# Two heads' scores in two neighbouring PSUM banks, one exponential over 1024 columns

## The chip, the cores and the metric

The kernel runs on one NeuronCore of one Trainium2 chip. The metric is the device time of one execution in microseconds, as the median of several runs. Next to it stands one profiled execution, whose span (first to last instruction) the views divide up.

## What is computed

A pre-norm transformer block on 2048 rows of 512 columns, in fp32: attention with 32 heads of 16 columns and no mask, then a feed-forward part with 1792 hidden columns and SiLU.

```python
def _A_ref(x, wqkv, wo):
    B, S, D = x.shape
    H = 32; Dh = D // H
    qkv = (lambda x, *d: x.transpose(*d))((x @ wqkv).reshape(B, S, 3, H, Dh), 2, 0, 3, 1, 4)
    q, k, v = qkv[0], qkv[1], qkv[2]
    scale = Dh ** -0.5
    scores = jnp.einsum("bhqd,bhkd->bhqk", q, k) * scale
    p = _softmax(scores, axis=-1)
    o = jnp.einsum("bhqk,bhkd->bhqd", p, v)
    return (lambda x, *d: x.transpose(*d))(o, 0, 2, 1, 3).reshape(B, S, D) @ wo
...
def _B_ref(x, w1, w2):
    h = jnp.einsum("bsd,df->bsf", x, w1)
    h = _silu(h)
    out = jnp.einsum("bsf,fd->bsd", h, w2)
    return out
...
h = x + _A_ref(_layernorm(x, axis=-1), A_wqkv, A_wo)
h2 = h + _B_ref(_layernorm(h, axis=-1), B_w1, B_w2)
```

## The kernel before

**Stages.** A first stage normalizes x, turns it and projects q, k and v. Q and k are stored as fp16 parts in DRAM, v stays in SBUF (`va`). Then the attention runs over 32 *items*. An item is a block of 512 query rows (four blocks, eight items each) and four heads; its 2048 keys are cut into 16 chunks. One item and one chunk make a *group*, so there are 512 groups. After the first group of items 9, 17 and 25 the feed-forward part of the finished block is run (`finish_block`, `mlp`), and that of the last block at the end (`finish_last`).

**A group.** The loop from line 690 writes the order out by hand; TensorE (PE), ScalarE (ACT), VectorE (DVE) and the DMA queue of SyncE (SP) each keep program order. Per group:

- `scores(g, k)` (line 459) for four heads: a matmul with 64 rows and 512 columns into a bank, and an exponential of 512 columns from that bank into a tile `pt` (ACT). Heads alternate between the lower and the upper half of PE's rows.
- `one_max` (line 257) after the first n of the four: a maximum needs the scores of later items, 128 queries by 512 keys, in an orientation of its own (a matmul with 48 rows on the *other* half of PE's rows, then a `tensor_reduce` on DVE). 64 of them make an item. `maxima(g)` (line 674) plans n, at most 3 a group, from what is done and from two constants, `BESIDE` and `AHEAD`.
- `values(g - 2)` (line 470): four fp32 matmuls of `pt` with `va`, 17 output rows each, side by side in the one bank `pv`. Each is two passes in the trace.

**Around the groups.** After an item's 64th maximum `finish_max` (line 210) reduces them to `nm` on DVE and splits it on POOL; two groups later `place_max` (line 223) transposes it on PE into a bank `ps_n`, copies it on ACT (`mt`), and sends it with four DMAs into the rows of `qs` that the item's scores read. After an item's last `values`, `finish_item` (line 485) copies `pv` on ACT (`pvs`), and the next item's `values` can begin only then. In items 8, 16 and 24, groups 10 to 15 carry `output` (line 618): twelve matmuls of the output projection into `ps_wo` (`project_rows`), an addition and statistics on DVE (`add_rows`), a normalization, and four transposes into `ps_tr` (`turn`, line 161), which ACT copies and from which DVE takes the low part.

**Banks.** PSUM has eight banks. From line 437 they are cut into rings: `st` with four banks (scores, `ps_n`, `ps_wo`, `ps_tr`, and the sums of `mlp`), `sm` with three (maxima; in `mlp` also `ps_n`), and `pv`. A ring hands its banks out in turn, so that a new user waits for the last reader of the oldest one.

**Feed-forward.** `mlp` (line 570) takes 14 chunks of 128 hidden columns; every eighth of its products is followed by a burst of three maxima.

Of the kernel before, what the change touches and what calls it, by code (L numbers as in the profile page):

```python
# [9 lines left out]
F32 = mybir.dt.float32  # L10
# [9 lines left out]
P = 128  # L20
# [17 lines left out]


LAG = 2  # L40
PTS = 12

RING = 5

# [1 line left out]
ITEMS = NB * H // 4  # L46

WAIT = 2
AHEAD = 4


BESIDE = 126
OUTPUT = 9

BESIDE_A = 7, 4
# [4 lines left out]
def attention_mlp_kernel(ctx: ExitStack, tc: tile.TileContext, x, wqkv, wo, w1, w2, out):  # L60
# [59 lines left out]
    def bank(name, kind="st", dtype=F32):  # L120
        return banks[kind].tile([P, 512], dtype, tag=kind, name=name)

    ident = const.tile([P, P], F32, name="ident")
    make_identity(nc, ident)
    ident_h = const.tile([P, P], F16, name="ident_h")
# [32 lines left out]
    def normalize(dst, rows, mv, rs):  # L158
        dve("tensor_scalar", dst, rows, mv[:, 0:1], rs, op0=ALU.subtract, op1=ALU.mult)

    def turn(src, dst_h, dst_l):

        ps = bank("ps_tr").rearrange("p (c n) -> p c n", n=P)
        for c in range(4):
            tr(ps[:, c, :], src[:, c * P:(c + 1) * P], ident)
        act("copy", dst_h, ps)
        low(dst_l, ps, dst_h)
# [54 lines left out]

    def place_max(i, ns):

        ps = bank("ps_n", "sm" if at["mlp"] else "st", F16)
        tr(ps[:32, :P], ns.rearrange("p a b -> p (a b)"), ident_h)
        mt = small.tile([32, P], F16, name="mt")
        pin(nc.scalar.copy(mt, ps[:32, :P]))
        for j in range(2):
            for r in range(2):  # L230
                dst = qs[i % RING][64 * j + 48 + r:64 * j + 49 + r].rearrange("o a n -> o (a n)")
                pin(nc.sync.dma_start(dst.rearrange("o (a b) -> o a b", b=P),
                                      mt[16 * r + 8 * j:16 * r + 8 * j + 8, :]))
        placed.add(i)
# [2 lines left out]
    todo = {(i, j): [(i, kb, qt, a, j) for kb in range(4) for a in range(2) for qt in range(4)]  # L237
            for i in range(ITEMS) for j in range(2)}
    END = 64 * ITEMS
    at = {"item": 0, "done": 0, "half": 0, "products": 0, "step": 0, "due": 0, "mlp": False}  # L240
    agenda = {}

    def soon(steps, fn, *a):
# [190 lines left out]
                    load_k(2 + n // 4, n % 4)  # L434


    open_banks(ctx, 1, st=4, sm=3, pv=1)
    pv = bank("pv", "pv")
    pin(nc.vector.memset(pv, 0.0))
    cpool = ctx.enter_context(tc.tile_pool(name="cpool", bufs=1, side="right"))  # L440
# [8 lines left out]
    groups = ITEMS * KC  # L449
    pts, den = {}, {}  # L450

    def scores(g, k):

        i, c = divmod(g, KC)
        a, j = HEADS[k]
        assert i in placed
        ps = bank("ps_s")
        mm(ps, ks[i % RING][64 * j:64 * j + 64, a, c * P:(c + 1) * P], qs[i % RING][64 * j:64 * j + 64, a, :],
           start=True, stop=True)
        pts[g, k] = bp.tile([P, 512], F32, name="pt")  # L460
        act("activation", pts[g, k], ps, AF.Exp, scale=qk_f)

    def values(g):
        i, c = divmod(g, KC)
        for k in range(4):
            a, j = HEADS[k]
            mm(pv[32 * k:32 * k + DH + 1, :], va[:, c, 4 * (i % 8) + 2 * a + j, :], pts.pop((g, k)),
               start=c == 0, stop=c == KC - 1)
        if c == KC - 1:
            finish_item(i)  # L470

# [93 lines left out]
        return statistics(h)  # L565

    def turn_rows(t):
        turn(hx.pop(t), hth[:, :, t * P:(t + 1) * P], htl[:, :, t * P:(t + 1) * P])

    def mlp(b, beside):  # L570
        engine = "pool" if beside else "dve"

        first = bank("ps_w1")
        acc = [bank("ps_acc") for _ in range(3)]

        def second(f, gh, gl):
            w2h, w2l = ws.pop(("w2", f))
            if f == 0:
                acc.append(bank("ps_acc"))
            for t in range(4):  # L580
                weave(product(acc[t], lambda c: gh[:, t * P:(t + 1) * P], lambda c: gl[:, t * P:(t + 1) * P],
                              lambda c: w2h, lambda c: w2l, 1, start=f == 0, stop=f == FC - 1),
                      beside if f < FC - 1 else None)
                if f == FC - 1:
                    n = 4 * b + t
                    h = rows_of(b, t)
                    dve("tensor_tensor", h, acc[t], h, ALU.add)
                    dma(out[n * P:(n + 1) * P, :], h)

        last = None  # L590
        for f in range(FC):
            tick()
            if f < 2:
                at["products"] = 12
            load_weights("w1", f + 2)
            load_weights("w2", f + 1)
            w1h, w1l = (w.rearrange("p (c n) -> p c n", n=P) for w in ws.pop(("w1", f)))
            split_weights("w1", f + 1, engine)
            split_weights("w2", f, engine)
            ps = pv if f else first  # L600
            weave(product(ps, lambda c: w1h[:, c, :], lambda c: w1l[:, c, :],
                          lambda c: hth[:, c, :], lambda c: htl[:, c, :], DC), beside)
            g, gh, gl = (bp.tile([P, 512], dt, tag="pt", name=name)
                         for name, dt in (("g", F32), ("gh", F32R), ("gl", F32R)))
            act("activation", g, ps, AF.Silu)
            act("copy", gh, g)
            low(gl, g, gh)
            if last:
                second(*last)
            last = (f, gh, gl)  # L610
        if b < NB - 1:

            act("activation", small.tile([P, 1], F32, name="sw"), ident[:, :1], AF.Exp)
        second(*last)
# [3 lines left out]
    def output(b, n):  # L618

        if n < 4:  # L620
            ps = bank("ps_wo")
            run(project_rows(n, ps))
            found[n] = add_rows(b, n, ps)
        if 0 < n < 5:
            normalize(hx[n - 1], rows_of(b, n - 1), *found.pop(n - 1))
        if 1 < n < 6:
            turn_rows(n - 2)

    def finish_block(b, pending):

        act("activation", small.tile([P, 1], F32, name="sw"), ident[:, :1], AF.Silu)
        for g in pending:
            values(g)
        at["mlp"] = True
        mlp(b, BESIDE_C)
        at["mlp"] = False

    def finish_last(pending):

        b, i = NB - 1, ITEMS - 1  # L640
        O = ot[b % 2]
        for t in range(4):
            os[t] = [bp.tile([P, DC, P], F32R, tag="pt", name=name) for name in ("oh", "ol")]
            act("copy", os[t][0][:, :3], O[:, t, :3])
            low(os[t][1][:, :3], O[:, t, :3], os[t][0][:, :3])
        for g in pending:
            values(g)
        agenda.clear()
        sums(i)
        invert(i)  # L650
        spread(i)
        split_weights("w1", 0, "dve")
        ps = [bank("ps_wo") for _ in range(4)]
        for t in range(4):
            run(project_rows(t, ps[t], range(3), stop=False))
        divide(i)
        for t in range(4):
            act("copy", os[t][0][:, 3:], O[:, t, 3:])
            low(os[t][1][:, 3:], O[:, t, 3:], os[t][0][:, 3:])
        act("activation", small.tile([P, 1], F32, name="sw"), ident[:, :1], AF.Silu)  # L660
        found = {}
        for t in range(4):
            run(project_rows(t, ps[t], [3], start=False))
            found[t] = add_rows(b, t, ps[t])
            if t > 0:
                normalize(hx[t - 1], rows_of(b, t - 1), *found[t - 1])
        normalize(hx[3], rows_of(b, 3), *found[3])
        for t in range(4):
            turn_rows(t)
        mlp(b, None)  # L670
# [19 lines left out]
    for g in range(groups):  # L690
        tick()
        i, c = divmod(g, KC)
        if g in marks:
            finish_block(i // 8 - 1, (g - 2, g - 1))
        if i + RING - 1 < ITEMS and 6 <= c < 14:
            (load_k if c % 2 else load_q)(i + RING - 1, c // 2 - 3)
        if g < DC:
            w = gp.tile([P, 512], F32, tag="w", name="w", bufs=4)
            dma(w, wo[g * P:(g + 1) * P, :])
            soon(8, split_wo, g, w)  # L700
        if i in (8, 16, 24):
            b, n = i // 8 - 1, c - OUTPUT
            if c < 4:
                load_rows(b, c)
            if c in first_weights:
                load_weights(*first_weights[c])
            if 0 <= n < 4:
                split_rows(b, n)
            if c == 13:
                split_weights("w1", 0, "pool")  # L710
        if g == groups - 4:
            for t in range(4):
                load_rows(NB - 1, t)
            for w in first_weights.values():
                load_weights(*w)
        n = maxima(g)
        for m in range(4):
            k = m ^ (g % 2)
            scores(g, k)
            if m < n:  # L720
                one_max(1 - HEADS[k][1])
        if i in (8, 16, 24) and c > OUTPUT:
            output(i // 8 - 1, c - OUTPUT - 1)
        if g - LAG >= 0 and not (g in marks or g - 1 in marks):
            values(g - LAG)
    assert at["done"] == END
# [33 lines left out]
```

## Time and profile before

| what | value |
|---|---|
| median of 3 runs | 1741.3 us (1739.5 to 1748.47) |
| profiled execution, its own time | 1747.01 us |
| its span; mean granted clock | 1745.2 us; 0.987 |
| PE, DVE, ACT, POOL busy | 1696.8, 1453.6, 1258.9, 229.5 us |
| groups of block 0 and item 8 (207.6 to 486.2 us) | 278.60 us; PE 275.74, DVE 257.79, ACT 277.34 busy |
| next block (627.7 to 877 us) | 249.30 us; PE 247.53, DVE 233.21, ACT 245.21 busy |
| next block (1017 to 1272 us) | 255.00 us; PE 249.33, DVE 233.41, ACT 245.51 busy |
| last block (1411 to 1632 us) | 221.00 us; PE 218.67, DVE 173.94, ACT 220.08 busy |

The first stage fills what lies before 207.6 us, and the feed-forward parts with the output projections what lies between these stretches. An engine counts as busy from an instruction's start to its end, with what overlaps counted once; ends of matmuls are modelled. In a row of the timeline stand start, length, engine, line, operation, output and inputs, shape, the number of merged instructions, and in brackets the idle time before and what ended it. A row with a count over one runs from the first one's start to the last one's end, and matmuls on the two halves of PE's rows overlap.

### The profile page before, as it was taken

How to read it: one execution, taken by the hardware profiler on the slowest of the kernel's cores; microseconds unless marked ns; L12 is line 12 of the kernel's file. 1: busy time of each engine (PE TensorE's matmuls, PEld its weight loads, DVE VectorE, ACT ScalarE, POOL GpSimd, SP SyncE). 2: the span in 40 equal slices, each digit the busy share in tenths (PEclk: the TensorE clock that was granted, in tenths of full speed). 3: DMA queues.
4: the chain of work that ended last, by engine and by line, in shares of the span. 5: the costliest groups of instructions: out<-in, count | busy, mean ns of one | idle time of the engine just before them, and what ended most of it. 6: DMA issues, size and time to landing. Idle time of an engine off the chain costs nothing.

```text
span 1745.2 us, 28284 instructions
## 1 busy us (share of the span) xinstructions
PE 1696.8 (97%) x10466; PEld 655.6 (38%) x10466; DVE 1453.6 (83%) x2392; ACT 1258.9 (72%) x2507; POOL 229.5 (13%) x312
## 2 busy tenths in 40 slices
PE   7899999999999999999999999999999999999899
PEld 6665422222245532222245532222245532221377
DVE  6879899999978889999978889999878899995243
ACT  4223499999963269999963369999863279999643
POOL 2112210000033300000033300000033300000000
PEclk9999999999999999999999999999999999999999
DMA  5234311111113111111222111111122111100232
GB/s 183 92 79 145 112 34 46 39 42 44 59 55 93 55 41 38 35 50 36 61 69 82 50 44 35 38 47 38 57 62 84 55 41 39 35 8 11 64 91 73
DMA packets 102211, 103.11 MB, mean 59 GB/s; under 512 B 20344, under 2 KB 78776, under 8 KB 102072
## 3 DMA queue, kind: packets, MB, share of 16 engines
q1 hardware_dynamic: 102072, 101.30, 19.6%
q8 instruction: 82, 1.34, 0.3%
q14 instruction: 57, 0.47, 0.1%
HBM read 77.86 MB, written 17.30 MB: 55 GB/s over the span
## 4 chain that ended last, share of the span: by engine, by line
ACT 45%; PE 44%; DVE 8%; DMA 1%; issue 1%; SPq 1%; POOL 0%; ACTq 0%; POOLq 0%; DVEq 0%
ACT pt L81 44%; PE pv L67 15%; PE ps_acc L67 7%; PE ps_m L67 6%; PE ps_qk L67 6%; DVE mx L206 5%; PE ps_s L67 5%; PE ps_wo L67 2%; PE ps_v L67 2%; DVE gl L84 1%; PE ps_w L67 1%; ACT pvs L81 1%; PE ps_tr L70 1%; DVE st L84 0%; DVE ot L84 0%
## 5 line engine op out<-in xcount | busy, mean ns | idle before, releaser
L206 DVE TENSOR_REDUCE mx<-ps_m 128x1 f32<-128x512 f32 x2048 | 1280.8, 683 | 127.5 <-PE ps_m L67 100.5
L81 ACT ACTIVATE pt<-ps_s 128x512 f32<-128x512 f32 x2048 | 1015.5, 657 | 34.8 <-PE ps_m L67 34.1
L67 PE MATMUL ps_s<-qs,ks 64*128 64x512 f16 x2048 | 552.7, 381 | 14.9 <-DMA qs<-mt 4.7
L67 PE MATMUL pv<-pt,va 128*17 128x512 f32 x4096 | 542.5, 603 | 0.8
L67 PE MATMUL ps_m<-ks,qs 48*128 48x512 f16 x2048 | 526.0, 383 | 2.2 <-DVE mx L206 0.8
L67 PEld LDWEIGHTS <-ks 64*128 64x128 f16 x2048 | 154.7, 95 | 552.3 <-issue 436.4
L67 PEld LDWEIGHTS pv<-pt,va 128*17 128x17 f32 x4096 | 68.7, 95 | 234.5 <-issue 219.7
L67 PEld LDWEIGHTS <-qs 48*128 48x128 f16 x2048 | 121.4, 94 | 77.0 <-issue 74.5
L81 ACT ACTIVATE g<-pv 128x512 f32<-128x512 f32 x52 | 31.0, 597 | 140.5 <-PE pv L67 140.4
L74 POOL TENSOR_SCALAR nm<-nm 128x16 f32<-128x16 f32 x32 | 9.4, 294 | 728.8 <-DVE nm L213 712.1
L67 PE MATMUL ps_acc<-w2h,gh 128*128 128x512 f32 x224 | 92.2, 411 | 0.0
L67 PE MATMUL ps_acc<-w2l,gh 128*128 128x512 f32 x224 | 91.6, 409 | 0.0
L67 PE MATMUL ps_acc<-w2h,gl 128*128 128x512 f32 x224 | 88.2, 394 | 0.0
L84 DVE TENSOR_TENSOR gl<-g,gh 128x512 fp32r<-128x512 f32 x56 | 53.3, 952 | 41.6 <-ACT gh L81 41.6
L67 PE MATMUL pv<-hth,w1l 128*128 128x512 f32 x208 | 86.2, 415 | 0.0
L81 ACT CAST w2h<-w 128x512 fp32r<-128x512 f32 x56 | 34.7, 620 | 70.7 <-PE ps_acc L67 33.9
L67 PE MATMUL pv<-hth,w1h 128*128 128x512 f32 x208 | 83.1, 400 | 0.0
L67 PE MATMUL pv<-htl,w1h 128*128 128x512 f32 x208 | 82.5, 397 | 0.0
L74 POOL TENSOR_TENSOR w1l<-w,w1h 128x512 fp32r<-128x512 f32 x42 | 53.7, 1280 | 154.6 <-ACT w1h L81 138.6
L81 ACT ACTIVATE ks<-ps_qk,qk_s 128x512 f32<-128x512 f32 x24 | 16.5, 688 | 68.2 <-PE ps_qk L67 68.2
L74 POOL TENSOR_TENSOR w2l<-w,w2h 128x512 fp32r<-128x512 f32 x42 | 53.7, 1280 | 50.1 <-ACT w2h L81 50.1
L67 PE MATMUL ps_qk<-xtl,wqk_h 128*128 128x512 f32 x128 | 53.4, 417 | 3.4 <-DVE xtl L84 3.4
(100 smaller groups left out, 1183.0 us busy)
## 6 DMA issues: line engine op xcount, KB each, us to landing
w<-in_B_w_dram SPq DMA_DIRECT2D x112, 256.0 KB
ks<-kd SPq DMA_DIRECT2D x120, 192.0 KB
qs<-qd SPq DMA_DIRECT2D x128, 48.0 KB
kd<-sh SPq DMA_DIRECT2D x16, 256.0 KB
qd<-sh SPq DMA_DIRECT2D x16, 256.0 KB
ot<-pvs SPq DMA_DIRECT2D x128, 32.0 KB
den<-dr SPq DMA_DIRECT2D x128, 32.0 KB
hx<-in_A_x_dram SPq DMA_DIRECT2D x16, 256.0 KB
```

What stands on the lines that cost most here:

```text
L67: tc.keep_in_program_order(nc.tensor.matmul(*a, **k))
L70: tc.keep_in_program_order(nc.tensor.transpose(*a))
L74: tc.keep_in_program_order(getattr(nc.gpsimd, op)(*a, **k))
L81: pin(getattr(nc.scalar, fn)(*a, **k))
L84: pin(getattr(nc.vector, fn)(*a, **k))
L206: pin(nc.vector.tensor_reduce(mx[i][:, j, a, qt, kb:kb + 1], ps, axis=AX.X, op=ALU.max))
```

## The change

Scores of two heads go into one tile of two neighbouring banks, and one exponential of 1024 columns reads both. The ring `st` of four banks becomes a ring `two` of two such tiles; the bytes of `pt` stay (six tiles of twice the size for twelve). A group's order becomes: pair of scores, up to two maxima, pair of scores, `output` if any, third maximum, `values`. `ps_n`, `ps_wo` and `ps_tr` move into the ring `sm` of three banks, which the maxima use. `mlp` and `finish_last` take their four sums from two such tiles. `mlp` runs one more burst of three maxima beside its first chunk (`BESIDE` 129 for 126), and `AHEAD` is 6 for 4.

```diff
-PTS = 12
+PTS = 6
...
-AHEAD = 4
-BESIDE = 126
+AHEAD = 6
+BESIDE = 129
...
+    def two_banks(name):
+        return banks["two"].tile([P, 2, 512], F32, tag="two", name=name)
...
-    def turn(src, dst_h, dst_l):
-        ps = bank("ps_tr").rearrange("p (c n) -> p c n", n=P)
+    def turn(src, dst_h, dst_l, kind="st"):
+        ps = bank("ps_tr", kind).rearrange("p (c n) -> p c n", n=P)
...
-        ps = bank("ps_n", "sm" if at["mlp"] else "st", F16)
+        ps = bank("ps_n", "sm" if "two" in banks else "st", F16)
...
-    open_banks(ctx, 1, st=4, sm=3, pv=1)
+    open_banks(ctx, 1, two=2, sm=3, pv=1)
...
-    def scores(g, k):
+    def scores(g, pair):
         i, c = divmod(g, KC)
-        a, j = HEADS[k]
         assert i in placed
-        ps = bank("ps_s")
-        mm(ps, ks[i % RING][64 * j:64 * j + 64, a, c * P:(c + 1) * P], qs[i % RING][64 * j:64 * j + 64, a, :],
-           start=True, stop=True)
-        pts[g, k] = bp.tile([P, 512], F32, name="pt")
-        act("activation", pts[g, k], ps, AF.Exp, scale=qk_f)
+        ps = two_banks("ps_s")
+        for m in range(2):
+            n = m ^ (g % 2)
+            a, j = HEADS[2 * pair + n]
+            mm(ps[:, n, :], ks[i % RING][64 * j:64 * j + 64, a, c * P:(c + 1) * P],
+               qs[i % RING][64 * j:64 * j + 64, a, :], start=True, stop=True)
+        pts[g, pair] = bp.tile([P, 2, 512], F32, tag="pt", name="pt")
+        act("activation", pts[g, pair], ps, AF.Exp, scale=qk_f)
...
-            mm(pv[32 * k:32 * k + DH + 1, :], va[:, c, 4 * (i % 8) + 2 * a + j, :], pts.pop((g, k)),
-               start=c == 0, stop=c == KC - 1)
+            mm(pv[32 * k:32 * k + DH + 1, :], va[:, c, 4 * (i % 8) + 2 * a + j, :],
+               pts[g, k // 2][:, k % 2, :], start=c == 0, stop=c == KC - 1)
...
-        first = bank("ps_w1")
-        acc = [bank("ps_acc") for _ in range(3)]
+        acc = [ps[:, m, :] for ps in [two_banks("ps_acc") for _ in range(2)] for m in range(2)]
+        first = acc[3]
...
-            if f == 0:
-                acc.append(bank("ps_acc"))
...
+            if beside and f == 0:
+                burst(beside[1])
...
-            g, gh, gl = (bp.tile([P, 512], dt, tag="pt", name=name)
-                         for name, dt in (("g", F32), ("gh", F32R), ("gl", F32R)))
+            g = bp.tile([P, 2, 512], F32, tag="pt", name="g")[:, 0, :]
+            gs = bp.tile([P, 2, 512], F32R, tag="pt", name="gs")
+            gh, gl = gs[:, 0, :], gs[:, 1, :]
...
-            ps = bank("ps_wo")
+            ps = bank("ps_wo", "sm")
...
-        ps = [bank("ps_wo") for _ in range(4)]
+        ps = [w[:, m, :] for w in [two_banks("ps_wo") for _ in range(2)] for m in range(2)]
...
-        n = maxima(g)
-        for m in range(4):
-            k = m ^ (g % 2)
-            scores(g, k)
-            if m < n:
-                one_max(1 - HEADS[k][1])
+        halves = [HEADS[(m + g) % 2][1] for m in range(maxima(g))]
+        scores(g, 0)
+        for half in halves[:2]:
+            one_max(half)
+        scores(g, 1)
         if i in (8, 16, 24) and c > OUTPUT:
             output(i // 8 - 1, c - OUTPUT - 1)
+        for half in halves[2:]:
+            one_max(half)
         if g - LAG >= 0 and not (g in marks or g - 1 in marks):
             values(g - LAG)
```

More of the change, by code (lines that the diff above doesn't have):

```diff
@@ L239, in attention_mlp_kernel @@
     END = 64 * ITEMS
-    at = {"item": 0, "done": 0, "half": 0, "products": 0, "step": 0, "due": 0, "mlp": False}
+    at = {"item": 0, "done": 0, "half": 0, "products": 0, "step": 0, "due": 0}
     agenda = {}
@@ L466, in values @@
             a, j = HEADS[k]
-            mm(pv[32 * k:32 * k + DH + 1, :], va[:, c, 4 * (i % 8) + 2 * a + j, :], pts.pop((g, k)),
-               start=c == 0, stop=c == KC - 1)
+            mm(pv[32 * k:32 * k + DH + 1, :], va[:, c, 4 * (i % 8) + 2 * a + j, :],
+               pts[g, k // 2][:, k % 2, :], start=c == 0, stop=c == KC - 1)
+        for pair in range(2):
+            del pts[g, pair]
         if c == KC - 1:
@@ L567, in turn_rows @@
     def turn_rows(t):
-        turn(hx.pop(t), hth[:, :, t * P:(t + 1) * P], htl[:, :, t * P:(t + 1) * P])
+        turn(hx.pop(t), hth[:, :, t * P:(t + 1) * P], htl[:, :, t * P:(t + 1) * P], "sm")
     def mlp(b, beside):
         engine = "pool" if beside else "dve"
-        first = bank("ps_w1")
-        acc = [bank("ps_acc") for _ in range(3)]
+        acc = [ps[:, m, :] for ps in [two_banks("ps_acc") for _ in range(2)] for m in range(2)]
+        first = acc[3]
         def second(f, gh, gl):
             w2h, w2l = ws.pop(("w2", f))
-            if f == 0:
-                acc.append(bank("ps_acc"))
             for t in range(4):
@@ L633, in finish_block @@
             values(g)
-        at["mlp"] = True
         mlp(b, BESIDE_C)
-        at["mlp"] = False
     def finish_last(pending):
@@ L642, in finish_last @@
         for t in range(4):
-            os[t] = [bp.tile([P, DC, P], F32R, tag="pt", name=name) for name in ("oh", "ol")]
+            o = bp.tile([P, 2, DC, P], F32R, tag="pt", name="os")
+            os[t] = o[:, 0], o[:, 1]
             act("copy", os[t][0][:, :3], O[:, t, :3])
```

## The prediction, made before the changed kernel was run

> **What bounds the kernel now.** I read the page first: busy time by engine, then the chain of work that ended last.
>
> ```profile
> PE 1696.8 (97%) x10466; PEld 655.6 (38%) x10466; DVE 1453.6 (83%) x2392; ACT 1258.9 (72%) x2507; POOL 229.5 (13%) x312
> ...
> ACT pt L81 44%; PE pv L67 15%; PE ps_acc L67 7%; PE ps_m L67 6%; PE ps_qk L67 6%; DVE mx L206 5%; PE ps_s L67 5%; PE ps_wo L67 2%; PE ps_v L67 2%; DVE gl L84 1%; PE ps_w L67 1%; ACT pvs L81 1%; PE ps_tr L70 1%; DVE st L84 0%; DVE ot L84 0%
> ...
> L206 DVE TENSOR_REDUCE mx<-ps_m 128x1 f32<-128x512 f32 x2048 | 1280.8, 683 | 127.5 <-PE ps_m L67 100.5
> L81 ACT ACTIVATE pt<-ps_s 128x512 f32<-128x512 f32 x2048 | 1015.5, 657 | 34.8 <-PE ps_m L67 34.1
> ```
>
> The chain names the exponentials (44%), but PE is busy for 97%. Which of the two sets a group's pace is not to be read from shares, so I took the timeline of PE through one ordinary group with three maxima, and of ACT through groups with none.
>
> ```profile
> 704.46 0.39 PE L67 MATMUL ps_s<-qs,ks 64*128 64x512 f16 x1
> 704.46 0.60 PE L67 MATMUL ps_m<-ks,qs 48*128 48x512 f16 x2
> 704.69 0.59 PE L67 MATMUL ps_s<-qs,ks 64*128 64x512 f16 x2
> ...
> 705.13 0.37 PE L67 MATMUL ps_s<-qs,ks 64*128 64x512 f16 x1
> 705.43 1.05 PE L67 MATMUL pv<-pt,va 128*17 128x512 f32 x8
> 706.42 0.39 PE L67 MATMUL ps_s<-qs,ks 64*128 64x512 f16 x1
> ...
> 1612.42 17.85 ACT L81 ACTIVATE pt<-ps_s 128x512 f32<-128x512 f32 x36
> ```
>
> A group lasts 706.42 - 704.46 = 1.96 us. PE fills it: seven short matmuls in four slots of 0.22 (two run side by side on the two halves of the rows, the last alone), `values` 0.97 after the start, and 0.99 to the next group. ACT: 36 exponentials in 17.85 us are one every (17.85 - 0.66) / 35 = 0.491, so four take 1.96 too. **Both limits coincide.** Whatever ACT saves, a group with three maxima cannot be shorter than PE's 1.96. Following the planner's arithmetic, 489 of the 512 groups carry three maxima before, 486 after.
>
> **The steady group.** PE's order after: pair at 0, two maxima at 0.22, pair at 0.45, third maximum at 0.67, `values` at 0.97, next group at 1.96: the same four slots. Nothing is removed on PE. On ACT two instructions replace four; their price isn't in the trace, so I bound it by what columns cost in neighbouring shapes.
>
> ```profile
> L81 ACT CAST gh<-g 128x512 fp32r<-128x512 f32 x56 | 34.8, 621 | 1.8
> L81 ACT ACTIVATE g<-pv 128x512 f32<-128x512 f32 x52 | 31.0, 597 | 140.5 <-PE pv L67 140.4
> L81 ACT ACTIVATE sw<-ident 128x1 f32<-128x1 f32 x7 | 1.4, 203 | 0.1
> L81 ACT CAST oh<-ot 128x128 fp32r<-128x128 f32 x4 | 0.9, 295 | 10.3 <-DVE ot L84 10.3
> ```
>
> ```profile
> 502.89 0.39 PE L67 MATMUL ps_s<-qs,ks 64*128 64x512 f16 x1
> ...
> 503.31 0.60 ACT L81 ACTIVATE pt<-ps_s 128x512 f32<-128x512 f32 x1 [0.20 <-PE ps_m L67]
> ```
>
> Columns cost (597 - 203) / 511 = 0.77 ns or (621 - 295) / 384 = 0.85 ns, so 512 more cost 0.395 to 0.435 us. An exponential by itself takes 0.60; one of 1024 columns then lasts D = 0.995 to 1.035 and comes every I = 0.886 to 0.926. ACT needs 2I = 1.77 to 1.85 a group: some 0.15 idle, the real gain of this change.
>
> But only two tiles exist, and they tie ACT to PE. The first exponential starts 0.42 after its scores (502.89 to 503.31), the second ends at 0.42 + D + I, the next group's second pair may start 0.05 later (bank handed on, shown below), and from there PE needs 1.96 - 0.45 = 1.51 to the next group. Two periods are thus at least 0.42 + D + I + 0.05 + 1.51, or P = (1.98 + D + I) / 2. With D + I = 1.88 to 1.96 that gives 1.93 to 1.97: at PE's own 1.96, and over it by up to 0.01. For some 430 ordinary groups 0 to +4 us; I take **+2**.
>
> The Trainium skill, "ScalarE: Activation LUTs", section "What ACT_TABLE_LOAD costs", gives an ACTIVATE with immediate operands 186 ns plus 0.833 ns a column, overlapping the next by about 93 ns. Estimated from it, D + I is 1.04 + 0.95 = 1.99, P 1.985 and this term +11 us; but for 512 columns it gives one every 520 ns, where the trace has 491, so I keep the rows.
>
> **The end of an item.** Its copy of `pv` stands between exponentials on ACT.
>
> ```profile
> 342.30 0.39 PE L67 MATMUL ps_s<-qs,ks 64*128 64x512 f16 x1
> ...
> 343.36 1.05 PE L67 MATMUL pv<-pt,va 128*17 128x512 f32 x8
> ...
> 346.62 0.39 PE L67 MATMUL ps_s<-qs,ks 64*128 64x512 f16 x1
> ```
>
> ```profile
> 342.69 0.62 ACT L81 COPY pvs<-pv 128x512 f32<-128x512 f32 x1
> 343.15 4.09 ACT L81 ACTIVATE pt<-ps_s 128x512 f32<-128x512 f32 x8
> ```
>
> `pvs` ends at 343.31 and `values` starts at 343.36: this is the 0.05 of handing on. The two groups take 4.32, 0.40 over 3.92. After: the copy takes ACT 0.46 (342.69 to 343.15), of which the 0.15 of idle time covers a part; 0.31 is left and delays the second pair. 28 such ends: **-2** (-11 if all of it were covered, 0 if none).
>
> **`ps_n` among the maxima.** This wait is new.
>
> ```profile
> 372.10 0.39 PE L67 MATMUL ps_s<-qs,ks 64*128 64x512 f16 x1
> ...
> 374.40 0.39 PE L67 MATMUL ps_s<-qs,ks 64*128 64x512 f16 x1
> ...
> 375.29 0.37 PE L67 MATMUL ps_s<-qs,ks 64*128 64x512 f16 x1
> ```
>
> ```profile
> 372.13 2.47 DVE L206 TENSOR_REDUCE mx<-ps_m 128x1 f32<-128x512 f32 x4
> ```
>
> ```profile
> 374.98 0.25 ACT L228 COPY mt<-ps_n 32x128 f16<-32x128 f16 x1
> ```
>
> The copy `mt` ends at 375.23, and the fourth score, whose turn it is for that bank, starts at 375.29: rings hand out strictly in turn. Before, this cost some 0.2, often nothing. After, `ps_n` takes the first of three maxima banks, so the second maximum needs the bank of the group before's third. DVE reduces one every (2.47 - 0.68) / 3 = 0.60: beginning 0.22 + 0.42 into a group it ends the third at 2.52, or 0.56 into the next. The second maximum waits until 0.61 instead of 0.22, and behind it in PE's order stand the second pair, the third maximum and `values`: 0.39, against about 0.1 before. 23 items are placed inside groups: **+7** (0 to +9). The wait of 372.10 to 374.40 (2.30) is the item's last reduction `nm` on DVE; it stays.
>
> **`output` among the maxima.**
>
> ```profile
> 486.19 0.39 PE L67 MATMUL ps_s<-qs,ks 64*128 64x512 f16 x1
> ...
> 492.35 0.39 PE L67 MATMUL ps_s<-qs,ks 64*128 64x512 f16 x1
> ...
> 497.40 0.39 PE L67 MATMUL ps_s<-qs,ks 64*128 64x512 f16 x1
> ...
> 508.87 0.39 PE L67 MATMUL ps_s<-qs,ks 64*128 64x512 f16 x1
> ```
>
> ```profile
> 488.37 0.50 PE L67 MATMUL ps_wo<-wo_h,oh 128*128 128x512 f32 x1 [0.63 <-ACT pt L81]
> ```
>
> ```profile
> 501.63 0.69 DVE L84 TENSOR_TENSOR ot<-ps_wo,hx 128x512 f32<-128x512 f32 x1 [1.19 <-POOL ol L74]
> ...
> 503.19 0.52 DVE L84 TENSOR_SCALAR hx<-ot,mv,rs 128x512 f32<-128x512 f32 x1
> ```
>
> Four groups take 6.16, 5.05, 5.49 and 5.98 (502.89 stands above). In the first the projection waits for an exponential's bank (488.37); that wait, about 0.9, goes. But the third maximum is now reduced behind the projection's whole chain on DVE (501.63 to 503.71, 2.1), so its bank is free 2.1 + 0.7 = 2.8 after the projection. PE is back at the next projection after 0.30 + 0.99 + 0.67, with turns about 2.2. That is 0.6 in each of four groups, and a lone maximum between projection and `values` adds a slot of 0.22 in three: 2.4 + 0.7 - 0.9 = 2.2 a block, less what DVE catches up; three blocks: **+5** (-3 to +9).
>
> **More maxima beside `mlp`.**
>
> ```profile
> 559.82 0.60 PE L67 MATMUL ps_m<-ks,qs 48*128 48x512 f16 x3
> 560.35 0.50 PE L67 MATMUL ps_acc<-w2l,gh 128*128 128x512 f32 x1
> ```
>
> A burst costs 0.53; three are added, **+1.5**. Item 24's maxima end two groups earlier for it (group 380 instead of 382). That matters:
>
> ```profile
> 1241.41 0.39 PE L67 MATMUL ps_s<-qs,ks 64*128 64x512 f16 x1
> ...
> 1248.07 0.58 PE L67 MATMUL ps_s<-qs,ks 64*128 64x512 f16 x1 [4.28 <-DMA qs<-mt]
> ...
> 1254.29 0.39 PE L67 MATMUL ps_s<-qs,ks 64*128 64x512 f16 x1
> ```
>
> Three groups take 12.88 instead of 5.88, since the four DMAs of `mt` land late and PE then runs slowly for a while (0.58 for 0.39). SP issues them 3.92 earlier, so 0.4 of the 4.28 is left, too short for the slow stretch: **-6** (-7 to 0). `AHEAD` changes nothing: the plan is at its cap of three.
>
> **Groups without maxima.** At the end 24 groups have none. PE lacks the third maximum's slot, so P = (1.98 - 0.22 + 1.92) / 2 = 1.84 for 1.96: **-3**.
>
> **Starts.**
>
> ```profile
> 628.10 5.99 ACT L81 ACTIVATE pt<-ps_s 128x512 f32<-128x512 f32 x12 [4.56 <-PE ps_m L67]
> ```
>
> Four times three groups start with ACT alone on the path: 12 x 0.49 becomes 6 x 0.91, 0.4 less: **-2**. The last four turns go through three banks instead of four, about +0.5. Tiles of `pt` keep their bytes and their distance of three groups; in `mlp` two of six tiles a chunk still leave the chunk before its own: nothing.
>
> **Sum:** 2 - 2 + 7 + 5 + 1.5 - 6 - 3 - 2 + 0.5 = **+3 us**. The profiled execution took 1747.0, its span and 1.8 around it, so 1750 by it; the median, 5.7 below, becomes **1744**. Its own range, from the bounds of the terms: 1733 to 1755.
>
> **Rivals.**
>
> *The pair's chain decides (slower).* Above D + I = 1.94 each 0.01 costs 0.005 a group, 2.2 us in all. If the fixed part is not saved, D = 1.20 and I = 0.98, P is 2.08 and the term +52. For: exponentials under load last 0.66, not 0.60, on average, and nothing in the trace crosses a bank. Against: both slopes above. Halfway to the bound from 1.92, D + I = 2.05, P 2.015 and +24: **1766**. The page's rule named above lies on this path, at about 1753; 0.06 of this rival's chance is for it.
>
> *ACT's idle time takes the ends of items (faster).* If the two tiles run further apart than I reckon, the copy hides: -11 instead of -2; if DVE also has its third maximum done earlier, `ps_n` and `output` cost nothing: 2 - 11 + 1.5 - 6 - 3 - 2 + 0.5 = -18: **1723**. For: ACT gets 0.15 a group back. Against: 0.31 over two groups must then come from a loop that is full at 1.96.
>
> *It doesn't do what it says:* the two matmuls of a pair don't run side by side. 0.22 twice in 486 groups, over +200. Against: three maxima in 0.60 (559.82) need only two slots.
>
> **Chances.** Forecast 0.52, slower rival 0.26, faster rival 0.20, the last 0.02. A measurement can tell about 0.5%, 8.7 us: faster means below 1732.6, slower above 1750.0. Faster: 0.20 and 0.04 of the forecast, 0.24. Slower: 0.28 and 0.10 of it, 0.38. Within: 0.38. The range reaches to 1722, the faster rival, and 1765, the middle of the slower one; about a tenth is left out on each side.
>
> **What would show it.** Ordinary groups of 1.96 to 1.97, with ACT idle for 0.1 to 0.2 in each, show the steady step right; above 1.98 the slower rival is at work, and exponentials over 1.04 long say why. In groups that begin behind a `ps_n`, the second maximum should wait for DVE by 0.4. After item 24's start there should be no row with a wait for `mt` above 1 us. I am wrong if ordinary groups fall below 1.95, since PE's slots then aren't what I take them for.

## The result, and the profile after

The changed kernel takes **1760.8 us** (median of 4 runs, 1760.2 to 1762.9), beside 1741.0 for the kernel before on the same chip: ratio 1.0103, 95% interval 1.0085 to 1.0122. It is slower by 1%. (All ratios here are to the kernel before on the same chip; they differ a little from the ratio of the two medians.) The profiled execution took 1762.9, its span and 1.8 around it. The forecast was 1744 in a range of 1722 to 1765: the range holds the time, but the change came out slower, on the side of the slower rival, and the forecast's own mechanism didn't hold, as the last sections show.

The page of after, busy time by engine, the chain of waits and three groups (group, shape, count, busy us, mean ns, idle time before it and what ended that):

```profile
PE 1696.2 (96%) x10466; PEld 650.1 (37%) x10466; DVE 1456.1 (83%) x2392; ACT 1236.7 (70%) x1483; POOL 229.7 (13%) x312
...
PE 66%; DVE 13%; ACT 11%; issue 7%; DMA 1%; POOL 1%; SPq 1%; ACTq 0%; POOLq 0%; DVEq 0%
...
L209 DVE TENSOR_REDUCE mx<-ps_m 128x1 f32<-128x512 f32 x2048 | 1281.4, 684 | 122.5 <-PE ps_m L67 88.5
L81 ACT ACTIVATE pt<-ps_s 128x1024 f32<-128x1024 f32 x1024 | 989.6, 1026 | 66.6 <-PE ps_s L67 45.3
...
L67 PE MATMUL ps_acc<-w2h,gs 128*128 128x512 f32 x448 | 144.8, 405 | 6.3 <-DVE ot L84 6.3
```

ACT issues 1024 exponentials for 2048 and is busy for 22 us less. The chain that named the exponentials for 44% before now names PE for 66% and ACT for 11%. So the relief that the change gives to ACT is real, yet the span grew by 15.9. The timeline of PE through three ordinary groups of after, and of ACT at one exponential in the first:

```profile
355.43 0.39 PE L67 MATMUL ps_s<-qs,ks 64*128 64x512 f16 x2
355.66 0.38 PE L67 MATMUL ps_m<-ks,qs 48*128 48x512 f16 x2
355.88 0.39 PE L67 MATMUL ps_s<-qs,ks 64*128 64x512 f16 x2
356.10 0.38 PE L67 MATMUL ps_m<-ks,qs 48*128 48x512 f16 x1
356.40 1.05 PE L67 MATMUL pv<-pt,va 128*17 128x512 f32 x8
357.39 0.39 PE L67 MATMUL ps_s<-qs,ks 64*128 64x512 f16 x2
...
357.92 0.39 PE L67 MATMUL ps_s<-qs,ks 64*128 64x512 f16 x2
...
359.42 0.39 PE L67 MATMUL ps_s<-qs,ks 64*128 64x512 f16 x2
```

```profile
355.93 1.02 ACT L81 ACTIVATE pt<-ps_s 128x1024 f32<-128x1024 f32 x1
```

PE's four slots are there as forecast (0, 0.23, 0.45, 0.67), but groups alternate: 357.39 - 355.43 = 1.96, then 359.42 - 357.39 = 2.03. In the second the second pair starts 0.53 after the first and not 0.45, since it waits for its tile. And the exponential, 1.02 long, starts 0.50 after its scores (355.93 - 355.43). In the kernel before that was 0.42. Over all ordinary groups the median is 0.497 in after and 0.423 in before.

Six such groups as one window (stretch, its length, then busy time of PE, PEld, DVE, ACT and POOL with counts, granted clock, DMA share, GB/s), first after, then before:

```profile
355.43:367.41 11.98, 11.98 (x94) 2.63 (x91) 11.32 (x19) 11.63 (x13) 1.28 (x1) 1.00 0.31 74
```

```profile
746.51:758.27 11.76, 11.76 (x94) 2.64 (x92) 11.32 (x19) 11.76 (x26) 1.28 (x1) 1.00 0.17 66
```

11.98 / 6 = 1.997 a group for 1.960, and ACT, which was busy without a gap, idles for 0.06 a group (the forecast sign was 0.1 to 0.2). Some 430 ordinary groups, the prediction's estimate, make about +16: as much as the whole difference.

That the sum comes out so is partly chance, since other stages moved too. The second large one is `mlp`, which runs ahead of the first group of items 9, 17 and 25 and not behind it, as was said above: from the first scores of the group ahead of it to those of the group behind it 119.05, 119.17 and 119.07 for 115.67, 115.65 and 115.43, +10.5. Its last chunk, on PE and DVE of after and on DVE of before:

```profile
632.00 0.73 PE L67 MATMUL ps_acc<-w2h,gs 128*128 128x512 f32 x2 [0.78 <-DVE ot L84]
...
634.45 0.73 PE L67 MATMUL ps_acc<-w2h,gs 128*128 128x512 f32 x2 [0.78 <-DVE ot L84]
```

```profile
631.26 0.69 DVE L84 TENSOR_TENSOR ot<-ps_acc,ot 128x512 f32<-128x512 f32 x1
633.01 1.39 DVE L84 TENSOR_TENSOR ot<-ps_acc,ot 128x512 f32<-128x512 f32 x2 [1.06 <-PE ps_acc L67]
635.45 0.69 DVE L84 TENSOR_TENSOR ot<-ps_acc,ot 128x512 f32<-128x512 f32 x1 [1.05 <-PE ps_acc L67]
```

```profile
625.73 2.74 DVE L84 TENSOR_TENSOR ot<-ps_acc,ot 128x512 f32<-128x512 f32 x4
```

Before, four additions ran straight through. After, the products of sum 1 wait until DVE has added sum 0, and those of sum 3 until it has added sum 2: each pair of sums is one tile, and PE may not write in a tile that DVE has yet to read. The prediction doesn't speak of it.

PE's waits by cause, whole span, after and then before (us in total, times, longest):

```profile
PE ps_s L67 <- ACT pt L81: 13.6, 55, 0.9
...
PE ps_acc L67 <- DVE ot L84: 6.3, 8, 0.8
...
PE ps_wo L67 <- DVE mx L209: 3.2, 6, 0.8
...
PE ps_s L67 <- DMA qs<-mt: 0.3, 1, 0.3
```

```profile
PE ps_s L67 <- DMA qs<-mt: 4.7, 2, 4.3
...
PE ps_s L67 <- ACT pt L81: 2.2, 8, 0.5
PE ps_wo L67 <- ACT pt L81: 1.9, 3, 0.6
```

The long wait for `mt` at item 24's start is gone, as forecast. The projection no longer waits for an exponential's bank, but for one that DVE reduces a maximum from. The alternating 0.08 of the ordinary groups isn't in the 13.6: those 55 waits stand at ends of items, at starts, in `output` and in the groups without maxima. The modelled ends of matmuls cover the 0.08, so that PE counts as busy for all of the 11.98. A wait that small is seen in the starts alone.

### The profile page after: what moved, and what is told of

It reads as the page before. It is cut to its first block, busy times and chain, and to the rows that moved or that the text cites. A ratio compares the mean times of both kernels' runs of the same rounds, so it can differ in the third digit from the quotient of the medians.

```text
span 1761.1 us, 28220 instructions
## 1 busy us (share of the span) xinstructions
PE 1696.2 (96%) x10466; PEld 650.1 (37%) x10466; DVE 1456.1 (83%) x2392; ACT 1236.7 (70%) x1483; POOL 229.7 (13%) x312
## 4 chain that ended last, share of the span: by engine, by line
PE 66%; DVE 13%; ACT 11%; issue 7%; DMA 1%; POOL 1%; SPq 1%; ACTq 0%; POOLq 0%; DVEq 0%
PE pv L67 27%; PE ps_m L67 13%; PE ps_s L67 12%; ACT pt L81 11%; DVE mx L209 8%; PE ps_acc L67 7%; PE ps_qk L67 6%; DVE gs L84 2%; DVE ot L84 1%; PE ps_v L67 1%; DVE st L84 1%; POOL ol L74 1%; DMA ks<-in_A_x_dram 1%; SPq L87 0%; POOL rs L74 0%
## 5 line engine op out<-in xcount | busy, mean ns | idle before, releaser
L81 ACT ACTIVATE pt<-ps_s 128x1024 f32<-128x1024 f32 x1024 | 989.6, 1026 | 66.6 <-PE ps_s L67 45.3
L67 PE MATMUL ps_m<-ks,qs 48*128 48x512 f16 x2048 | 492.7, 379 | 7.4 <-DVE htl L84 3.2
L67 PE MATMUL ps_s<-qs,ks 64*128 64x512 f16 x2048 | 406.6, 384 | 16.9 <-ACT pt L81 13.6
L67 PEld LDWEIGHTS <-ks 64*128 64x128 f16 x2048 | 140.3, 93 | 590.6 <-issue 513.8
L67 PE MATMUL ps_acc<-w2h,gs 128*128 128x512 f32 x448 | 144.8, 405 | 6.3 <-DVE ot L84 6.3
L67 PEld LDWEIGHTS <-qs 48*128 48x128 f16 x2048 | 114.4, 94 | 71.0 <-issue 69.3
L67 PEld LDWEIGHTS ps_acc<-w2h,gs 128*128 128x128 f32 x448 | 80.4, 188 | 40.1 <-issue 16.1
L67 PE MATMUL ps_acc<-w2l,gs 128*128 128x512 f32 x224 | 91.6, 409 | 0.0
L84 DVE TENSOR_TENSOR gs<-g,gs 128x512 fp32r<-128x512 f32 x56 | 55.3, 988 | 41.7 <-ACT gs L81 41.7
```

Of the source, the lines that this page charges most:

```text
L67: tc.keep_in_program_order(nc.tensor.matmul(*a, **k))
L81: pin(getattr(nc.scalar, fn)(*a, **k))
L84: pin(getattr(nc.vector, fn)(*a, **k))
```

## The experiments

**Theory after the first look.** The exponential starts 0.07 later than the forecast had it, and the tie between the two tiles turns that into time. Why 0.07: in the compiled program an exponential of after has two waits, one for PE and one for ACT itself, for the exponential six before that filled the same `pt` tile. An exponential there carries one wait, so the wait for PE stands on an instruction of its own ahead of it (EventSemaphore) on ACT's queue; the traces of after and before have 1290 and 294 such on ACT. The one ahead of the exponential at 355.93 starts at 355.86, 0.43 after the scores. **Rival:** scores in neighbouring banks, or 1024 columns, make the start late whatever is waited for. `mlp` was to be split into the extra burst and the shared tiles.

**e1, the wait moved off the critical exponential.**

```diff
-        act("activation", pts[g, pair], ps, AF.Exp, scale=qk_f)
+        e = exps[g, pair] = nc.scalar.activation(pts[g, pair], ps, AF.Exp, scale=qk_f)
+        pin(e)
+        if pair and (g - 1, 0) in exps:
+            tc.add_manual_dep(e.ins, exps[g - 1, 0].ins.name, ...)
```

The second exponential of a group now waits for an exponential that covers what the next group's first would have waited for, so that one is left with PE alone. ACT's trace has 802 of the extra instructions for 1290.

> One part of the changed kernel is altered: the wait of an exponential for the exponential six before it, which wrote the same tile, is taken off the first exponential of a group and met by the second one, which waits for a later one anyway. Theory (own-engine wait): in the changed kernel the first exponential starts 0.49 us after its scores instead of 0.42, since its two waits need an instruction of their own ahead of it; the loop through the two tiles charges half of these 0.07 to every group. Groups then go from 1.997 to 1.96 on average, some 430 of them: 1760.8 becomes about 1746. Rival (the long exponential itself, its length plus its spacing, makes the loop): the start may move, the period stays at 1.99 to 2.00 and the time at 1758 to 1762.

Measured: 1748.0 (1746.5 to 1751.8) beside 1743.2, ratio to before 1.0030 (1.0017 to 1.0042). The window of the same six groups, the first scores in it, and their exponential:

```profile
351.27:363.05 11.78, 11.78 (x94) 2.63 (x90) 11.32 (x19) 11.63 (x13) 1.28 (x1) 1.00 0.33 74
```

```profile
351.27 0.39 PE L67 MATMUL ps_s<-qs,ks 64*128 64x512 f16 x2
```

```profile
351.71 1.02 ACT L466 ACTIVATE pt<-ps_s 128x1024 f32<-128x1024 f32 x1
```

1.963 a group for 1.997, with ACT's busy time unchanged. The exponential, 1.02 long as in after, starts 0.43 after its scores (0.44 by the rounded rows; the median over ordinary groups is 0.432), just when the extra instruction started in after. The late start is the cause, worth 1.0103 - 1.0030 of 1742, 12.7 us (give or take 4, estimated from the two intervals); neither the banks nor the columns are, since both stayed. e10 shows the same from the other side.

**e2, the sums of `mlp` taken in the order A0, B0, A1, B1**, so that consecutive sums lie in different tiles (the same for the last block's projection):

```diff
-        acc = [ps[:, m, :] for ps in [two_banks("ps_acc") for _ in range(2)] for m in range(2)]
+        tiles = [two_banks("ps_acc") for _ in range(2)]
+        acc = [ps[:, m, :] for m in range(2) for ps in tiles]
```

> One part of the changed kernel is altered: of the four sums of the feed-forward part and of the last output projection, neighbours in time lie in different two-bank tiles (order A0, B0, A1, B1 instead of A0, A1, B0, B1). Theory (shared tile): in the last chunk the matmuls of sum 1 and 3 wait for the addition that reads sum 0 and 2 of the same tile, 0.95 each; two in each of three blocks, two at the end, and two in the last projection: 1760.8 becomes about 1752, and each feed-forward stretch of 119.1 becomes about 117.2. Rival (the three maxima added to each block make the longer stretch): no change, 1759 to 1762.

Measured: 1755.0 (1752.3 to 1758.6), ratio 1.0068 (1.0047 to 1.0090), 6 us less than after (give or take 5, estimated from the two intervals). DVE at the end of `mlp` in e2:

```profile
629.12 1.37 DVE L84 TENSOR_TENSOR ot<-ps_acc,ot 128x512 f32<-128x512 f32 x2
630.87 1.39 DVE L84 TENSOR_TENSOR ot<-ps_acc,ot 128x512 f32<-128x512 f32 x2 [0.38 <-PE ps_acc L67]
```

One gap of 0.38 is left of two of 1.05, so the theory holds; `mlp` takes 117.4 to 117.6, and the end of the last block, 116.4 in after, 113.5.

**e3, both edits.**

> Both alterations together. If both theories hold the gains add up: about -15 and -9, near 1737, below the kernel before. If both rivals hold: 1758 to 1762.

Measured: 1742.8 (1740.8 to 1745.1), ratio 0.9995 (0.9983 to 1.0008). The gains add (12.7 + 6.1 of 18.8), and both theories hold, though their gains were put at 15 and 9. With both edits the change as a whole neither gains nor loses against the kernel before. That isn't the worth of the pair of heads alone: e3 still holds the earlier maxima, which by themselves gain 0.2% (e7), and `output` among the maxima, which by itself costs 0.1% (e6). The pair without these was not run.

**e4, the pair of banks kept and two exponentials of 512 columns** over it:

```diff
-        act("activation", pts[g, pair], ps, AF.Exp, scale=qk_f)
+        for m in range(2):
+            n = m ^ (g % 2)
+            act("activation", pts[g, pair][:, n, :], ps[:, n, :], AF.Exp, scale=qk_f)
```

> The changed kernel with one part undone: the two-bank tiles stay, but two exponentials of 512 columns read them. Theory (the loop through two tiles sets the group): a tile's second exponential ends 0.42 + 0.60 + 3 x 0.49 = 2.49 after the group's start, the next pair can follow 0.05 later, and with 1.51 to the next group two periods are 4.05, so 2.03 a group: about 1775, slower than with the long exponential. Rival (the long exponential is what costs time, the tiles of two banks are harmless): groups return to 1.96 and the time to about 1745.

Measured: 1795.6 (1791.7 to 1796.8), ratio 1.0294 (1.0268 to 1.0320). That the tiles' tie costs time with four instructions is confirmed, its size was expected 20 us too low. Six groups:

```profile
355.34:367.70 12.36, 12.22 (x94) 2.63 (x91) 11.39 (x20) 12.07 (x26) 1.27 (x1) 1.00 0.29 64
```

Groups alternate between 1.96 and 2.16, 2.06 on the mean. The start is late by the same 0.07 here (0.50 on the median), which the expectation left out. A group's four exponentials take 2.065 from the first start to the last end (median), so the loop of two tiles is 0.497 + 2.065 + 0.05 + 1.51 = 4.12, or 2.06 a group. So in two tiles the long exponential is worth 33 us (1.0294 - 1.0103). In the four single banks of before a group already takes PE's 1.96, so there it would have nothing to gain; that was not run.

**e5, the kernel before with `ps_n` among the maxima**, and nothing else (`"sm" if "pv" in banks else "st"`).

> The kernel before, with one part of the change alone: ps_n takes its bank among the three banks of the maxima instead of among the four of the scores. First theory: the bank's turn among the maxima costs about 0.3 more than among the scores in each of the 23 items placed inside groups, as in the changed kernel, where a group with a placement is 0.25 to 0.3 over its neighbours; the time rises by 4 to 7 us, to about 1747. Rival: the last reduction of the item on DVE hides the wait, and the time stays where it is, within 2 us.

Measured: 1743.9 beside 1742.5, ratio 1.000 (0.999 to 1.001). The rival holds. Behind three of the 23 placements the next group grew by 0.22 (2.17 to 2.39), behind two by 0.09; most groups with a placement take 2.31, here and in the kernel before.

**e6, the kernel before with `ps_wo` and `ps_tr` among the maxima**, the third maximum still ahead of `output` (`bank("ps_wo", "sm")`, and `turn(..., kind="sm")` for the rows of `hx`).

> The kernel before, with ps_wo and ps_tr in the banks of the maxima, and nothing else: the third maximum stays ahead of output. The three output stretches of the changed kernel are 1.3 to 1.5 us longer each than before. First theory: the wait for a bank that DVE has yet to reduce makes them so, and they are longer by 1 to 2 here too, +3 to +6 us, about 1747. Rival: the third maximum's place behind output makes them so, and they stay at 25.8 here or get shorter by the bank that the projection no longer waits for; 0 to -3 us, about 1741.

Measured: 1746.1 beside 1742.5, ratio 1.0013 (1.0001 to 1.0025). The three output stretches are 1.4 to 1.5 longer each, in after 1.3 to 1.5, so the first theory holds for the stretches, though the time rose by 2.3 (0.2 to 4.4) where it named 3 to 6. PE in the second, third and fourth of the first block's output groups of e6:

```profile
491.19 0.51 PE L67 MATMUL ps_wo<-wo_h,oh 128*128 128x512 f32 x1 [0.40 <-DVE mx L206]
...
497.07 0.49 PE L67 MATMUL ps_wo<-wo_h,oh 128*128 128x512 f32 x1 [0.86 <-DVE mx L206]
...
502.95 0.37 PE L67 MATMUL ps_m<-ks,qs 48*128 48x512 f16 x1 [0.64 <-DVE htl L84]
```

Three maxima and a projection take turns in three banks within a group: the projection waits for a reduction, and from the fourth group on a maximum waits for `htl`, the last reader of the bank that the third group's turn took.

**e7, the kernel before with `BESIDE` 129, `AHEAD` 6 and the extra burst:**

```diff
+            if beside and f == 0:
+                burst(beside[1])
```

> The kernel before, with BESIDE 129, AHEAD 6 and the extra burst beside mlp's first chunk, and nothing else. First theory: the stall at the start of item 24, 7 to 9 us, goes as it did in the changed kernel, since its maxima end two groups earlier, and the three bursts cost 0.5 to 1.8 each; the time falls by 3 to 7 us, to about 1738. Rival: the gain at item 24 came from the new order of a group and not from the earlier maxima, and the bursts only cost: +2 to +5 us, about 1746.

Measured: **1739.4** (1737.3 to 1741.6) beside 1742.5, ratio 0.9978 (0.9968 to 0.9989). A small part of the change, alone, makes the kernel faster by 0.2%. The start of item 24, and the extra burst in the first `mlp`, on PE of e7:

```profile
1241.54 0.37 PE L67 MATMUL ps_s<-qs,ks 64*128 64x512 f16 x1 [0.36 <-DMA qs<-mt]
```

```profile
529.04 0.50 PE L67 MATMUL ps_m<-ks,qs 48*128 48x512 f16 x2
529.77 0.37 PE L67 MATMUL ps_m<-ks,qs 48*128 48x512 f16 x1 [0.23 <-DVE mx L206]
530.36 0.22 PE L70 MATMUL ps_n<-ident_h,ns 128*32 128x128 f16 x1 [0.22 <-DVE mx L206]
```

The wait for `mt` is 0.36 for 4.28. The forecast had worked out 0.4. A burst costs 1.4 to 1.9 in each `mlp` (117.03, 117.50 and 117.01): it stands four products behind the burst before it, DVE hasn't emptied the banks yet, and the third maximum waits, here `ps_n` too.

**e8, e3 with the third maximum ahead of `output`.**

> The changed kernel with the early wait of the first exponential and the sums of mlp in the order of e3, and the third maximum ahead of output instead of behind it. First theory: behind output the third maximum's reduction stands on DVE behind the projection's addition and statistics, and its bank comes late for the group after; ahead of it the output stretches fall from 27.3 to about 25.5, about -4 us on e3: 1738 to 1739. Rival: the banks of the maxima are held up by output in either order, and the time stays at e3's 1743.

Measured: 1743.7 beside 1742.5, ratio 0.9998 (0.9985 to 1.0010); the output stretches stay at 27.2 to 27.6. The rival holds: with the banks so divided, the order doesn't matter.

**e9, e7 without the burst in block 2's `mlp`** (`if beside and f == 0 and b < 2`).

> The kernel before with BESIDE 129, AHEAD 6 and the extra burst as in e7, but beside the feed-forward parts of blocks 0 and 1 only: that of block 2 comes after item 24's maxima. First theory: item 24's start stays as in e7 and the third feed-forward part gets back the 1.4 to 1.8 us that its burst cost: about 1737.7. Rival: the maxima that the burst took out of the last block's groups were worth as much there, and the time stays at e7's 1739.4.

Measured: 1741.0 beside 1744.2, ratio 0.9982 (0.9970 to 0.9995). e7 and e9 can't be told apart. The third `mlp` got back 1.1 (115.9 for 117.0), but the first four groups of items 17 and 25, which vary from run to run (below), took 3.2 more in this profile. Inconclusive.

**e10, the kernel before with the second wait added** to every exponential, on the exponential three before it:

```diff
+        exps.append(e)
+        if len(exps) > 3:
+            tc.add_manual_dep(e.ins, exps[-4].ins.name, ...)
```

> The kernel before, in which each exponential also waits for the exponential three before it, which has long ended; nothing else changes, and 1922 of the 2048 get the extra instruction on ACT's queue. First theory: the extra instruction is paid for only where an exponential has to wait for its scores, as in the loop of two tiles; in the kernel before with its four banks the exponentials follow each other without a gap, the extra instruction is taken while the one before runs, ordinary groups stay at 1.96, and the time rises by 0 to 4 us, about 1745. Rival: it costs 0.07 in each exponential wherever it stands, 0.28 a group: about 1870.

Measured: 1744.7 beside 1744.2, ratio 1.0005 (0.9995 to 1.0015). Six ordinary groups:

```profile
743.72:755.48 11.76, 11.76 (x94) 2.64 (x91) 11.32 (x19) 11.76 (x26) 1.28 (x1) 1.00 0.17 68
```

As in before, 11.76 for six. So the rival falls. But the first theory isn't quite right either. The first scores of a group and its first exponential, here and then in before:

```profile
747.64 0.39 PE L67 MATMUL ps_s<-qs,ks 64*128 64x512 f16 x1
...
748.13 0.62 ACT L461 ACTIVATE pt<-ps_s 128x512 f32<-128x512 f32 x1
```

```profile
748.47 0.39 PE L67 MATMUL ps_s<-qs,ks 64*128 64x512 f16 x1
...
748.89 0.69 ACT L81 ACTIVATE pt<-ps_s 128x512 f32<-128x512 f32 x1
```

A group's first exponential, which has to wait for its scores, starts 0.49 after them for 0.42: it is late by 0.07 in the four single banks too, with 512 columns. Over the ordinary groups the medians are 0.489 and 0.423. The three behind it follow as closely as before: from the first one's start to the last one's it is 1.45 in both. Thus an exponential pays for the extra instruction where it waits for its input, and not where it follows another one directly. What the 0.07 does to the period is a second matter: in the loop of two tiles PE waits for it, while in four banks the group stays at PE's 1.96. The Trainium skill, "Perfetto Trace Analysis", section "Identifying Dependency Chains", says that instructions that wait on several engines may have EventSemaphore instructions inserted ahead of them with the additional waits. The program and these runs agree, and add that ACT itself counts as one of these engines, and a price: 0.07 of the start or nothing, by where it stands.

## Where the prediction held and where it failed, by its own steps

| step | forecast | profile, after less before | runs |
|---|---|---|---|
| ordinary groups | +2 | +16 | e1 takes 12.7 back |
| ends of items | -2 | about -2 (from e3: 1.96 + 2.30 for 2.05 + 2.27) | none by itself |
| `ps_n` among maxima | +7 | about 0 (18 placements among ordinary groups: -0.3 in all) | e5: 0 (-2 to +2) |
| `output` among maxima | +5 | +4.3 | e6: +2.3 (0.2 to 4.4) |
| bursts, `mlp` | +1.5 | +10.5 | e7: 4.8 in its profile; e2 takes 4.8 back |
| item 24 | -6 | -6.5 (12.88 to 6.36) | e7: there too |
| no maxima | -3 | -1.4 | e3: -2.0 |
| starts after `mlp` | -2 | -6.2 | varies without the change |
| last block | +0.5 | +3.8 | e2, e3: +0.8 |

The column of the profile adds up to 18.5, where the span grew by 15.9; the first stage was 0.9 shorter, and the first two rows are estimates. That the range held the time owes something to luck: `ps_n`, put 7 too high, and the starts, 4 too high, made up for most of the 14 by which ordinary groups were put too low.

**The step that failed** is the start in the steady group: "The first exponential starts 0.42 after its scores (502.89 to 503.31)". It starts 0.50 after them. Everything else in that formula held: D 1.02 (forecast 0.995 to 1.035), I 0.92 (0.886 to 0.926), 0.05 to hand on, 1.51 to the next group. With 0.42 these give (1.98 + 1.94) / 2 = 1.96, what e1 measures (1.963); with 0.50 they give 2.00, what after measures (1.997). 0.42 was read off an exponential whose only wait was for PE, and carried over to one that has two. Thus the slower rival, the chain of the pair, decided, at its place and between the forecast's bound of 1.97 and its own 2.015, but not at its price: D + I is 1.94, just where the rival was to begin, and in ordinary groups most exponentials last 1.02, not over the 1.04 that was its sign.

The page that stood in the prediction, the Trainium skill's "ScalarE: Activation LUTs", section "What ACT_TABLE_LOAD costs", gave D 1.04 and I 0.95, and with them 1.985. The trace has 1.02 and 0.92, so the rows were the better source; that 1.985 lies nearer to 1.997 than my 1.96 is chance.

**`mlp`** is a term that was mis-sized twice: a burst was priced by one that follows the last at eight products' distance (0.53), but the added one follows at four, and finds banks full (1.4 to 1.9, e7); and of the sums' new tiles the prediction said nothing. A tile is waited for as a whole, so a tile of two banks ties two sums together that had been apart: two waits of 0.78 in each `mlp`, of which e2 takes most back. The same holds for the end (+3.8, 0.8 with the sums apart).

**`ps_n`** was priced by one place at which two waits overlapped. The price of 0.39 against 0.1 is not there: in e5 three groups grew by 0.22, two by 0.09 and the time by 0 (-2 to +2). The forecast sign in which the second maximum should wait for DVE by 0.4 is not there: PE's waits of `ps_m` for `mx` come to 2.0 us in the whole of after.

**`output`** came out in size, for half the reason given: the wait for an exponential's bank (1.9 in the three blocks) went as forecast, but what is paid for it is the projection's own wait for a bank of maxima (3.2) and a maximum's wait for `htl` (3.2 too), and not the third maximum's place behind the projection's chain (e6, e8).

**Item 24** went as worked out, and the "slow stretch" in it has a name in the windows of before and after, at the column behind POOL's count (granted clock):

```profile
1241.41:1254.29 12.88, 8.60 (x50) 1.83 (x47) 6.27 (x11) 6.68 (x15) 0.67 (x3) 0.73 0.14 42
```

```profile
1254.00:1260.36 6.36, 6.07 (x50) 1.36 (x47) 5.73 (x10) 5.87 (x7) 0.00 (x0) 1.00 0.27 87
```

With PE's wait of 4.28 the clock is 0.73 on the mean of the three groups; without the wait it stays at 1.00. Two parts of the wait in before, which lasted from 1243.79 to 1248.07:

```profile
1243.79:1246.10 2.31, 0.00 (x0) 0.00 (x0) 0.12 (x1) 0.31 (x2) 0.00 (x0) 1.00 0.01 1
1246.25:1248.07 1.82, 0.00 (x1) 0.03 (x2) 0.00 (x0) 0.00 (x0) 0.00 (x0) 0.50 0.04 11
```

The Trainium skill, "TensorE: Matmul & The Clock Gate", section "What's actually happening", has the clock halved after at least one idle window of about 3.4 us. This stretch agrees that the clock is halved in a wait of this length, but here it fell when PE had been idle for some 2.4 us. The clock is also why the starts after `mlp` were no fair term: the same four groups took 10.95 in the profile of before and 8.03 in that of e10, which alters only the waits of the exponentials, at mean clocks of 0.69 and 1.00:

```profile
627.68:638.63 10.95, 10.91 (x46) 2.42 (x45) 8.28 (x15) 8.05 (x16) 0.67 (x3) 0.69 0.23 83
```

```profile
627.31:635.34 8.03, 7.98 (x48) 2.19 (x48) 8.00 (x15) 7.61 (x16) 0.67 (x3) 1.00 0.30 113
```

What decides between the two there, no run shows. In the profiles of the kernels with four single banks 9 of 18 such starts were slowed like this, and 2 of 15 in those with the long exponential, so the change may make them rarer; that stays open. One such start moves a single profile by 2.9, which is why the verdicts above rest on ratios of many runs.

**No maxima:** with the late start these groups alternate too, 1.84 and 1.96, so that about half of the gain is lost. The first scores of three of them on PE of after (the first row merges two pairs):

```profile
1606.36 0.92 PE L67 MATMUL ps_s<-qs,ks 64*128 64x512 f16 x4
1608.20 0.39 PE L67 MATMUL ps_s<-qs,ks 64*128 64x512 f16 x2
...
1610.16 0.92 PE L67 MATMUL ps_s<-qs,ks 64*128 64x512 f16 x4
```

## What to carry to other kernels

When a change cuts the number of buffers between two engines to two, the time from the producer's start to the consumer's start goes into the period (here by half, since the loop spans two groups): read it off an instruction with the same waits as the new one, and count how many semaphores the new one waits for, its own engine's among them. A wait that can't be avoided belongs on an instruction that follows another one directly, and not on one that waits for fresh input. Tiles that are merged for one reader are merged for every other user of that ring: look at each of them (here the sums of `mlp`) before pricing the change at its target.

## What the runs showed of the hardware

- A second, long satisfied wait costs an ACTIVATE 0.07 us of its start where it waits for PE (medians of 0.497 in after and e4 and 0.489 in e10, for 0.432 in e1 and 0.423 in before), with 512 columns as with 1024, and nothing where it follows another ACTIVATE directly (e10).
- An exponential over two neighbouring banks is 1.02 long, and the next one starts 0.92 after it; those of 512 columns come every 0.49. Crossing the bank shows no cost: the 512 further columns take 0.42 (1.02 - 0.60), within the 0.395 to 0.435 that other shapes gave. What a merge saves is about 0.06 for each pair (0.98 - 0.92).
- A burst of three maxima costs 0.53 in PE's time at eight products behind the last one (before), and 1.4 to 1.9 at four (e7), where the third maximum waits for DVE, which reduces one bank every 0.60.
